# Padding the DRAM buffers between the two stages of an FFT convolution: 132 KB instead of 128 KB for each frequency pair

## The chip, the core and the metric

The kernel runs on one core of a Trainium2 chip. The metric is the device time of one execution in microseconds (us). Several runs are taken and the median is given. One further execution was recorded by the hardware profiler; the tables and lines of the profile come from that one.

## What is computed

```python
B, S, D = 8, 5696, 128                       # x: (B, S, D), h: (S, D), float32
Xf = np.fft.rfft(x, n=2 * S, axis=1)
Hf = np.fft.rfft(h, n=2 * S, axis=0)
y  = np.fft.irfft(Xf * Hf[None], n=2 * S, axis=1)[:, :S, :]
x  = y.reshape(B * S, D)                     # 45568 tokens
logits = x @ phi                             # phi: (128, 32), 8 experts with 4 slots
d = softmax of logits over the tokens; slot_input = d.T @ x
slot_out[e] = relu(slot_input[e] @ w1[e]) @ w2[e]
c = softmax of logits over the 32 slots;  out = c @ slot_out
```

It is a causal convolution along the sequence, done by a transform of twice the length, followed by a soft mixture of experts. All data are float32.

## The kernel before, in words

The sequence of 5696 tokens is seen as 89 rows of 64 columns. The transform has two factors, N1 = 90 and N2 = 64. It is applied to nine sequences in turn: first h (g = 0), then the eight batches of x (g = 1 to 8). Each sequence passes through three stages, and spectra travel between stages through DRAM.

**Stage A** (`load_x`, `fold`, `first_stage`) takes a chunk of 4 columns and their mirror image; NJ = 8 chunks make a sequence. `load_x` brings them in by two DMAs (80 rows and 9 rows). `fold` (line 206, GpSimd) forms sum and difference. `first_stage` multiplies by cosine and sine tables on TensorE (line 217), ScalarE copies the result from PSUM to the tile `fst` in SBUF (line 220, a ring of four), and SP stores it in DRAM (line 226). There are two shapes of stores. `first_low` holds two components of one chunk in partitions 0 to 63 and 64 to 127, of which 60 each are stored (two DMAs of 240 KB). `first_high`, in every odd step, holds two components of two chunks in four groups of 32 partitions, of which 30 each are stored (four DMAs of 120 KB). Each partition writes one run of 4 columns x 2 x 128 x 4 bytes = 4 KB.

**The DRAM buffer `fd[g]`** (line 131) holds the spectrum of one sequence after stage A: NP = 45 frequency pairs, in each pair 2 halves (`a`) of 64 columns (`r`), in each column 2 x 128 values. A column is 1 KB, a half 64 KB, a pair 128 KB. So the rows of one store, one for each half of each pair, are 64 KB apart. There are nine such buffers, one for each sequence, and none is used twice.

**Stage B** (`load_g`, `stage_b1`, `stage_b2`) transforms along the 64 columns. A unit is four pairs (NW = 12 units in a sequence, the last with one pair). `load_g` (line 253, SP) reads a unit into the tile `gt`, a ring of four: 128 partitions (half and column), 4 pairs, 1 KB each, 512 KB in all. TensorE multiplies (line 267), VectorE multiplies by the spectrum of h (lines 285 and 294), TensorE transforms back (line 309), ScalarE copies to `zst` (line 315), and SP stores it in `zd[b]` (line 318), which has the same pairs of 128 KB and is not changed.

**Stage C** (`load_pair`, `stage_c1` to `stage_c6`) reads 1 MB pieces of `zd` into `zc` (line 346), finishes the inverse transform (line 365), transposes (line 393), forms logits and keeps running sums of the softmax over tokens. After the last step the expert layers run and the output is written (lines 753 to 850).

**Order of the work.** It is written out by hand. One step of the main loop (line 583) handles one chunk of stage A, one or two units of stage B of the sequence before (LAG_B = 9 steps later) and, in every second step, one part of stage C (LAG_C = 27 steps later). Within a step two strings, `ORDER_E` and `ORDER_O` (line 581), give the order in which the pieces are issued: "x" loads x three steps ahead, "X" and "Y" are stage A with its stores, "p" and "P" prefetch units of stage B up to two steps ahead, "b" is a unit of stage B with its store, "z" loads for stage C. Nearly all DMAs are issued by SP, one after the other in this order; a DMA that has to wait holds up those behind it on SP. A load of a unit waits until all stores of the sequence that reach its pairs have landed.

Of the kernel before, what the change touches and what calls it, by code (L numbers as in the profile page):

```python
# [10 lines left out]
F32 = mybir.dt.float32  # L11
# [66 lines left out]
def kernel(  # L78
# [24 lines left out]
    nc = tc.nc  # L103
    P = 128
    B, S, D = x.shape
# [4 lines left out]
    N1, N2 = 90, 64  # L110
    R1, HALF, NP = S // N2, N2 // 2, N1 // 2
    CH = 4
# [15 lines left out]
    t_s1, t_i1, t_w, t_v, t_turn = [  # L128
        nc.inline_tensor(t, f"tab_{n}").ap()
        for n, t in zip(("s1", "i1", "w", "v", "turn"), transform_tables(S, N1, N2, CH, X0))]  # L130
    fd = [nc.dram_tensor(f"f_{g}", (NP, 2, N2, 2, D), F32, kind="Internal").ap() for g in range(B + 1)]
    zd = [nc.dram_tensor(f"z_{b}", (NP, 2 * N2, 2, D), F32, kind="Internal").ap() for b in range(B)]
    cd = nc.dram_tensor("c_t", (P, B * NQ, Q, 2, MH), F32, kind="Internal").ap()

# [38 lines left out]
    def bank():  # L173
        rings.append(rings.pop(0))
        return rings[-1].tile([P, 512], F32, name="bank", tag="bank")
# [34 lines left out]
    def first_stage(tiles, width):  # L210

        st = apool.tile([P, CH, 2, D], F32, name="fst", tag="fst", bufs=4)
        for G in range(2):
            p = bank()
            for o, (c, comp) in enumerate(tiles):
                k = slice(0, HP) if width == HP else slice(HP, HP + QP)
                nc.tensor.matmul(p[o * width:(o + 1) * width, :], s1[:, comp + G, k],  # L217
                                 folded[(c, comp)][:, :, :].rearrange("p n d -> p (n d)"),
                                 start=True, stop=True)
            nc.scalar.activation(st[:, :, G, :],  # L220
                                 p[:, :].rearrange("p (n d) -> p n d", d=D), AF.Copy)
        for o, (c, comp) in enumerate(tiles):
            g, j = divmod(c, NJ)
            n0 = comp * HALF + CH * j
            k0, n = (0, N1A) if width == HP else (N1A, N1 - N1A)
            nc.sync.dma_start(
                out=fd[g].rearrange("q a r c d -> (q a) (r c d)")[k0:k0 + n, n0 * 2 * D:(n0 + CH) * 2 * D],
                in_=st[o * width:o * width + n, :, :, :].rearrange("k n c d -> k (n c d)"))

    def first_low(c):  # L230
        first_stage([(c, comp) for comp in range(2)], HP)

    def first_high(c):

        both = [(c - 1 + i, comp) for i in range(2) for comp in range(2)]
        first_stage(both, QP)
        for b_ in both:
            del folded[b_]
# [3 lines left out]
    def parts(u):  # L242

        g, w = divmod(u, NW)
        return g, w, [(i, min(2, NP - 2 * i)) for i in range(2 * w, min(2 * w + 2, NU))]

    def load_g(u):
        if u >= (B + 1) * NW:
            return
        g, w, us = parts(u)  # L250
        n = sum(k for _, k in us)
        t_ = bpool.tile([P, 4, 2, D], F32, name="gt", tag="gt", bufs=4)
        nc.sync.dma_start(
            out=t_[:, 0:n, :, :].rearrange("p q c d -> p q (c d)"),
            in_=fd[g][4 * w:4 * w + n, :, :, :, :].rearrange("q a r c d -> (a r) q (c d)"))
        gs[u] = t_

    def stage_b1(u, share):
# [324 lines left out]
    for t in range(last_front + 1):  # L583
# [6 lines left out]
        def prefetch(last):  # L590
            nonlocal loaded
            while loaded < len(queue) and queue[loaded][1] <= last:
                load_g(queue[loaded][0])
                loaded += 1
# [58 lines left out]
        if NA < t <= NA + E:  # L653
# [13 lines left out]
                      in_=zring[0][held, :, :, :, :, :].rearrange("k h o n c d -> k (h o n c d)"))  # L667
# [16 lines left out]
    for q in range(Q):  # L684
        r = slice(q * NSL, (q + 1) * NSL)
        nc.gpsimd.tensor_copy(out=rep4[r, :, :],
                              in_=ident[r, r].unsqueeze(1).broadcast_to([NSL, Q, NSL]))
# [17 lines left out]
    for V in range(T, NT):  # L705
# [35 lines left out]
        else:  # L741
            for i in range(4 * (V - T - 1), min(4 * (V - T), E), 2):
                nc.sync.dma_start(
                    out=w2s[:, i:i + 2, :, :],
                    in_=moe_w2[i:i + 2].rearrange("e (p c) d -> p e c d", p=P))
# [39 lines left out]
    for g in range(EG):  # L785
        for k0 in range(0, NFC, 4):
            p = bank()
            for k in range(4):
# [3 lines left out]
                out=hidT[:, g, k0:k0 + 4, :], in_=p[:, :].rearrange("p (k c) -> p k c", k=4))  # L792
# [29 lines left out]
    for b in range(B):  # L822
        w1 = 0
        for n in (1, 2, 4, 4) if b == 0 else (4, 4, 3):
# [11 lines left out]
            for q in range(Q):  # L836
# [8 lines left out]
                out=ov[b, t0:t0 + n * RW * N2, :].rearrange("(w p n) d -> p w (n d)", p=P, n=CH),  # L845
                in_=o_[:, 0:n, :, :].rearrange("p w q d -> p w (q d)"))
            if lone:
                nc.sync.dma_start(
                    out=ov[:, NV * RW * N2:, :].rearrange("b (j n) d -> b j (n d)", n=CH),
                    in_=o_[:, n, :, :].rearrange("p q d -> p (q d)"))  # L850
# [29 lines left out]
```

## Time and profile before

| | |
|---|---|
| median of three runs | 871.69 us (867.33 to 872.01) |
| profiled execution, its own time | 869.39 us |
| its span, from first to last instruction | 867.6 us |
| mean granted TensorE clock | 0.947 of full speed |
| bytes moved by DMA | 272.46 MB, mean 314 GB/s |
| DMA pieces ("packets") | 156124, of which 113702 under 2 KB |
| HBM read, written | 142.81 MB, 128.21 MB |

How the profile is read: "busy" of an engine is the time in which it executed an instruction, and its share is of the span. A row of two dozen digits or more is the span in 40 equal slices, each digit the busy share in tenths, 9 for nine tenths or more. A group line gives the source line, the engine, the operation and the tiles as out<-in, then the number of instructions, then busy time and the mean of one. PEld is the loading of weights into TensorE, which overlaps with its matmuls (PE). The chain of work that ended last is followed back from the last instruction, at each step to what released it. "SPq" is SP's queue of instructions that issue DMAs; a DMA in the chain is the time from its issue to its landing.

The DMAs that touch the buffer, beside the largest others (KB each, number):

| DMA | number | KB each |
|---|---|---|
| f<-fst (line 226) | 144 and 144 | 240 and 120 |
| gt<-f (line 253) | 99 and 9 | 512 and 128 |
| z<-zst (line 318) | 88 and 8 | 512 and 128 |
| zc<-z (line 346) | 30, 90 and 30 | 1024, 128 and 32 |
| xc<-in_x_dram (line 195) | 64 and 64 | 320 and 36 |

### The profile page before, as it was taken

Reading aid. Unit: us, or ns where it says so; the run is one execution under the profiler, and the core shown is the slowest. Engines: PE = TensorE matmul, PEld = TensorE weight load, DVE = VectorE, ACT = ScalarE, POOL = GpSimd, SP = SyncE. Lnnn points to the kernel's source line nnn. Section 1 sums busy time; section 2 is a strip of 40 time slices with the busy share of each in tenths; the row PEclk is TensorE's granted clock in tenths of the full one; section 3 lists DMA queues with packets and bytes.
Section 4 is the critical chain, followed back from the end, with each engine's and each line's share of the span. In section 5 each row is a group of like instructions: output and inputs, shape, how many; then the busy total and the mean of one; then the engine's idle time right before and its main releaser. Section 6 shows DMA issues by size and latency. Waiting matters only on the chain.

```text
span 867.6 us, 20501 instructions
## 1 busy us (share of the span) xinstructions
PE 774.3 (89%) x7796; PEld 380.7 (44%) x7796; DVE 619.5 (71%) x929; ACT 442.6 (51%) x906; POOL 404.3 (47%) x386
## 2 busy tenths in 40 slices
PE   5889788889999999999999999999998888968993
PEld 1223333234444444444444444444454444444882
DVE  3049867667778778877888788777788895963642
ACT  2433244435555555655565565555544444773541
POOL 4453424245565566656566555555434332671000
PEclk9999999999999999999999999999999898988855
DMA  9899999999999999999999999999997886670898
GB/s 294 258 300 316 299 326 351 324 327 332 341 326 342 334 329 334 337 330 338 339 348 337 335 328 338 337 326 335 316 330 276 286 308 252 245 305 2 338 405 337
DMA packets 156124, 272.46 MB, mean 314 GB/s; under 512 B 12198, under 2 KB 113702, under 8 KB 152885
## 3 DMA queue, kind: packets, MB, share of 16 engines
q1 hardware_dynamic: 155451, 270.85, 90.2%
q8 instruction: 62, 1.02, 0.5%
q10 hardware_dynamic: 576, 0.31, 0.1%
q14 instruction: 35, 0.29, 0.1%
HBM read 142.81 MB, written 128.21 MB: 312 GB/s over the span
## 4 chain that ended last, share of the span: by engine, by line
PE 55%; DMA 20%; DVE 11%; SPq 2%; issue 2%; POOL 1%; ACT 1%; DVEq 0%; ACTq 0%
PE bank L365 13%; PE bank L217 11%; DMA zc<-z 8%; PE bank L309 7%; PE bt L267 7%; PE bank L393 6%; DMA out_dram<-o 4%; DMA xc<-in_x_dram 4%; DMA gt<-f 3%; DVE yf L294 3%; PE bank L480 3%; DVE p L285 2%; DVE bt L285 2%; SPq L346 2%; PE bank L431 2%
## 5 line engine op out<-in xcount | busy, mean ns | idle before, releaser
L206 POOL TENSOR_TENSOR x<-xc 128x512 f32<-128x512 f32 x144 | 180.1, 1275 | 228.5 <-PE bank L217 196.4
L217 PE MATMUL bank<-x,s 128*32 128x512 f32 (+1 forms) x1152 | 227.4, 613 | 16.3 <-POOL x L206 15.4
L315 ACT ACTIVATE zst<-bank 128x512 f32<-128x512 f32 (+1 forms) x184 | 98.7, 586 | 190.5 <-PE bank L309 168.8
L220 ACT ACTIVATE fst<-bank 128x512 f32<-128x512 f32 x216 | 127.5, 598 | 109.5 <-PE bank L217 85.0
L285 DVE TENSOR_TENSOR p<-bt,Hi 128x1024 f32<-128x1024 f32 x96 | 111.3, 1160 | 34.0 <-PE bt L267 33.1
L365 PE MATMUL bank<-zc,i 128*64 128x512 f32 x480 | 117.5, 611 | 10.8 <-DMA f<-fst 6.4
L309 PE MATMUL bank<-yf,vt 64*64 64x256 f32 x1440 | 102.4, 390 | 26.8 <-DVE yf L294 26.8
L217 PEld LDWEIGHTS bank<-x,s 128*32 128x32 f32 (+1 forms) x1152 | 57.0, 124 | 154.3 <-issue 76.1
L294 DVE TENSOR_TENSOR yf<-bt,p 128x512 f32<-128x512 f32 x192 | 119.3, 662 | 3.3
L267 PE MATMUL bt<-gt,wt 64*64 64x256 f32 x1620 | 113.7, 388 | 6.0 <-DMA gt<-f 3.9
L285 DVE TENSOR_TENSOR bt<-bt,Hr 128x1024 f32<-128x1024 f32 x96 | 112.9, 1177 | 0.0
L267 PEld LDWEIGHTS bt<-gt,wt 64*64 64x64 f32 x1620 | 54.0, 132 | 80.9 <-issue 38.0
L384 POOL TENSOR_TENSOR y<-y,op 128x512 f32<-128x512 f32 x64 | 77.5, 1211 | 11.4 <-DVE op L370 8.3
L309 PEld LDWEIGHTS bank<-yf,vt 64*64 64x64 f32 x1440 | 57.0, 135 | 58.0 <-issue 27.8
L370 DVE TENSOR_TENSOR y<-bank,y 128x512 f32<-128x512 f32 x32 | 22.1, 691 | 70.9 <-PE bank L365 70.6
L393 PE MATMUL bank<-ident,y 109*128 109x109 f32 x512 | 66.1, 283 | 0.7 <-DVE y L384 0.7
L384 POOL TENSOR_TENSOR y<-y,om 128x512 f32<-128x512 f32 x54 | 64.1, 1186 | 2.1
L365 PEld LDWEIGHTS bank<-zc,i 128*64 128x64 f32 x480 | 31.2, 137 | 74.6 <-issue 45.9
L393 PEld LDWEIGHTS bank<-ident,y 109*128 109x128 f32 x512 | 55.9, 154 | 16.5 <-issue 11.1
L395 ACT ACTIVATE yt<-bank 128x360 f32<-128x360 f32 x128 | 51.7, 489 | 4.2 <-PE bank L393 4.2
L833 PE MATMUL op<-so,cT 32*128 32x128 f32 x704 | 45.8, 378 | 3.6 <-ACT o L842 2.9
L285 DVE TENSOR_TENSOR p<-bt,turn 128x1024 f32<-128x1024 f32 (+1 forms) x12 | 14.2, 1179 | 46.6 <-PE bt L267 45.7
(97 smaller groups left out, 817.3 us busy)
## 6 DMA issues: line engine op xcount, KB each, us to landing
gt<-f SPq DMA_DIRECT2D x99, 512.0 KB
z<-zst SPq DMA_DIRECT2D x88, 512.0 KB
f<-fst SPq DMA_DIRECT2D x144, 240.0 KB
zc<-z SPq DMA_DIRECT2D x30, 1024.0 KB
xc<-in_x_dram SPq DMA_DIRECT2D x64, 320.0 KB
f<-fst SPq DMA_DIRECT2D x144, 120.0 KB
out_dram<-o SPq DMA_DIRECT2D x16, 1024.0 KB
zc<-z SPq DMA_DIRECT2D x90, 128.0 KB
```

Source lines behind the costliest of these rows:

```text
L206: nc.gpsimd.tensor_tensor(out=y_[:, :, :], in0=t_[:, 0, :, :], in1=t_[:, 1, ::-1, :], op=AL.subtract if comp else AL.add)
L217: nc.tensor.matmul(p[o * width:(o + 1) * width, :], s1[:, comp + G, k], folded[(c, comp)][:, :, :].rearrange("p n d -> p (n d)"), start=Tr ...
L220: nc.scalar.activation(st[:, :, G, :], p[:, :].rearrange("p (n d) -> p n d", d=D), AF.Copy)
L267: nc.tensor.matmul(bt[q * HP:(q + 1) * HP, a, o, :], wt[r, 2 * i + q, :], t_[r, 2 * o + q, :, :].rearrange("p c d -> p (c d)"), start=True ...
L285: nc.vector.tensor_tensor(out=p_, in0=pv, in1=h_, op=AL.mult)
L294: eng.tensor_tensor(out=y_[r, 0:k, c, :], in0=pv[:, :, c, :], in1=pi[r, 0:k, 1 - c, :], op=op_)
L309: nc.tensor.matmul(bz[q][a * HP:(a + 1) * HP, o * 2 * D:(o + 1) * 2 * D], vt[r, i, a, :], y_[r, a * m + o, :, :].rearrange("p c d -> p (c ...
L315: nc.scalar.activation(st[:, 0:m, q, :], bz[q][:, 0:m * 2 * D].rearrange("p (o x) -> p o x", o=m), AF.Copy)
L365: nc.tensor.matmul(p[h_ * HP:(h_ + 1) * HP, :], i1[0:kr, tab, :], t_[0:kr, h_, o, :, q, :], start=True, stop=True)
L384: eng.tensor_tensor(out=part_, in0=part(v, 0), in1=o_[:, :, :], op=sign)
L393: nc.tensor.transpose(p[:, i * TR:(i + 1) * TR], ys[T][0:TR, k * CH + i, 0:D], ident[0:TR, 0:TR])
L395: nc.scalar.activation(yt[:, k * CH:(k + 1) * CH, :, :], of_tokens(p), AF.Copy)
```

## The change

Each `fd[g]` is allocated with 4 more columns (4 KB) behind the 128 columns of each pair. The kernel works on the first 128 of each pair through a view; the 4 KB are never written or read. The distance from pair to pair becomes 132 KB. The distance between the halves of a pair stays 64 KB.

Because the two halves and the pairs no longer lie at one common distance, the destination of the stores in `first_stage` can't be written as one level of rows any more. It becomes two levels: pairs (30 for `first_low`, 15 for `first_high`) and halves (2), and then the run of 4 KB. The source in SBUF is written as before. The loads in `load_g` have halves and columns already joined in the view; their rows, pieces and sizes are the same. Nothing else is changed.

```diff
-    fd = [nc.dram_tensor(f"f_{g}", (NP, 2, N2, 2, D), F32, kind="Internal").ap() for g in range(B + 1)]
+    fd = [nc.dram_tensor(f"f_{g}", (NP, 2 * N2 + 4, 2, D), F32, kind="Internal").ap()[:, 0:2 * N2] for g in range(B + 1)]
...
             nc.sync.dma_start(
-                out=fd[g].rearrange("q a r c d -> (q a) (r c d)")[k0:k0 + n, n0 * 2 * D:(n0 + CH) * 2 * D],
+                out=fd[g].rearrange("q (a r) c d -> q a (r c d)", a=2)[
+                    k0 // 2:(k0 + n) // 2, :, n0 * 2 * D:(n0 + CH) * 2 * D],
                 in_=st[o * width:o * width + n, :, :, :].rearrange("k n c d -> k (n c d)"))
...
         nc.sync.dma_start(
             out=t_[:, 0:n, :, :].rearrange("p q c d -> p q (c d)"),
-            in_=fd[g][4 * w:4 * w + n, :, :, :, :].rearrange("q a r c d -> (a r) q (c d)"))
+            in_=fd[g][4 * w:4 * w + n, :, :, :].rearrange("q r c d -> r q (c d)"))
```

## Prediction

> **What bounds the kernel now.** I read the page first, then the stage table (busy time of each engine in chosen stretches), then the chain of work that ended last.
>
> ```profile
> span 867.6 us, 20501 instructions
> PE 774.3 (89%) x7796; PEld 380.7 (44%) x7796; DVE 619.5 (71%) x929; ACT 442.6 (51%) x906; POOL 404.3 (47%) x386
> DMA  9899999999999999999999999999997886670898
> ```
>
> Two resources look full: TensorE (89%) and the 16 DMA engines (nine tenths or more in most slices). The stage table shows which of them leads where. Its columns are the stretch and its length, busy us and instruction count of PE, PEld, DVE, ACT and POOL, then the granted clock, the DMA share and GB/s.
>
> ```profile
> 10.00:15.00 5.00, 5.00 (x15) 2.34 (x11) 0.00 (x0) 1.68 (x3) 2.00 (x2) 1.00 1.01 427
> 30.00:50.00 20.00, 16.38 (x73) 4.09 (x72) 0.00 (x0) 8.25 (x14) 11.00 (x9) 1.00 0.83 245
> 50.00:170.00 120.00, 101.61 (x906) 38.54 (x905) 93.17 (x106) 45.77 (x80) 45.01 (x36) 0.97 0.97 323
> 170.00:210.00 40.00, 34.54 (x298) 14.49 (x295) 25.91 (x36) 19.14 (x37) 18.94 (x17) 0.96 0.94 329
> 210.00:630.00 420.00, 412.86 (x4238) 191.74 (x4239) 332.78 (x514) 245.66 (x509) 240.35 (x223) 1.00 0.97 334
> 640.00:720.00 80.00, 67.08 (x741) 37.97 (x739) 69.40 (x108) 35.76 (x75) 27.41 (x28) 0.88 0.84 291
> ```
>
> From 210 to 630 us TensorE is busy 412.9 of 420 us: it sets the pace, and only 7.1 us are idle. The DMA share there is 0.97, so it just keeps up. From 50 to 210 us (the ramp, while the pipeline fills) TensorE is idle 160 - 101.6 - 34.5 = 23.9 us with the DMA share at 0.94 to 0.97. The last store to f is issued at 634 us, so nothing after about 700 us can be touched directly. The chain shows who leads in the ramp:
>
> ```profile
> 50.46 8.15 DMA xc<-in_x_dram
> 58.63 5.66 DMA gt<-f
> ...
> 74.41 7.89 DMA xc<-in_x_dram
> 82.37 5.42 DMA gt<-f
> ```
>
> Its share by line for 50 to 210 us is 19.9% loads of x, 16.9% loads gt<-f and 7.1% loads zc<-z: 44% of 160 us is 70 us of DMA in the chain. There the stores to f matter twice: they stand ahead of these loads on SP's one queue, and they share their DMA engines. Last, what issues cost (minimum, median, maximum in ns):
>
> ```profile
> L226 SPq DMA_DIRECT2D f<-fst x288: 314/362/1687, 13.9 to 634.3; - x144
> L253 SPq DMA_DIRECT2D gt<-f x108: 333/452/1426, 46.9 to 696.4; - x108
> ```
>
> **What the Trainium skill says.** (1) DMA: Bandwidth & Descriptors, Latency and other measured facts, row on HBM row pitch: copies of 16 KiB rows at a pitch of 512 KiB ran at 207 GB/s and at 4 MiB at 103; with 4 KiB added to the 4 MiB pitch 214. So the pad is of the size named there, but the pitch here is 64 KB in a pair and 128 KB between pairs, well under the one that lost only 3%. No view of this trace isolates such a loss. (2) The same page, Why a DMA increments its semaphore by 16 and not by 1: the number of engines is the largest number up to 16 that divides the slowest sizes of both sides. Before it is 60 and 60, and 30 and 30; after it 30 (pairs) and 60, and 15 and 30. All give 15, so the spread should not change. No view of the trace shows engines singly. (3) SBUF — State Buffer, Door 1: The DMA port swizzle: partitions 0 to 63 reach only 8 of 16 ports, and 1 MiB for 64 partitions was measured at 196 GB/s. This bears on a store whose 60 rows lie in one half of the partitions.
>
> Does the trace agree with (3)? In 30 to 50 us only x loads and f stores run. One round of two steps takes 8.89 us there (its first store is issued at 22.43, 31.32 and 40.21 us) and moves 0.73 MB of x and 1.47 MB of f. Busy time is 0.83 x 16 x 8.89 = 118 engine-us. At the 427 GB/s of the stretch that is full of table loads (26.7 GB/s for each engine) x would take 27. What is left, 91, over 360 pieces of 4 KB is about 252 ns a piece, where the table rate would give 153. Fifteen engines at 252 ns are 244 GB/s: stores to f are slow, and the 8 ports of (3), at 196 GB/s with the two halves partly overlapped, are enough to explain it. The pad does not touch ports.
>
> **The change part by part.** It removes nothing and adds no engine work, no bytes and no wait.
>
> (a) Stores (line 226, 288 of them). The pieces stay 60 or 30 of 4 KB. Their addresses go from multiples of 64 KB to pairs at 132 KB. Bounds of the unknown: if the pitch now costs as much as the page's 512 KiB (3% of 252 ns, 8 ns), the gain in the ramp is 87 stores (counted from their issues between 50 and 210 us) x 45 pieces on average x 8 ns / 16 = 2.0 us; if the new pitch is the worse one it is the same figure as a loss. With half of it on the path (44% of the ramp's chain is DMA) that is 0.9 us either way. I take -0.5 us, leaning to the page. From 210 to 630 us TensorE covers a gain, and a loss too as long as DMA slack lasts: 3% of a round of 20.3 us is 0.6 us, or 27 ns for each of the 22.5 pieces an engine has per round. Eight is below it.
>
> (b) Issue of the stores on SP. The destination gets a third level (pair, half, run) where it had two. No such row exists. The nearest is gt<-f with three levels: minimum 19 ns longer, median 90 ns longer, but it carries 512 pieces instead of 60. The lower end is nothing; a gain is excluded, since the pattern has no level fewer. I take 19 ns: 87 x 19 = 1.7 us in the ramp, half on the path 0.8 us; with 90 ns it is 3.9 us. In a round of the long stretch (456 to 476 us) SP's issues sum to about 16 us of 20.3, so eight stores at 19 or 90 ns more (0.2 or 0.7 us) lie in its 4 us of slack. Behind a store on SP stand the x load, z<-zst, and the zc and gt loads; a shift of 0.7 us meets loads that are issued one to two steps ahead.
>
> (c) Loads (line 253, 108 of them). The same 512 pieces of 1 KB, the same count on all levels; 128 rows on both sides before and after. Four pairs that were one run of 512 KB become four runs of 128 KB. Nothing in the page prices that; I take zero, with the same 3% as both ends. A piece may lengthen by 6.8 ns (0.6 us over 90 pieces an engine per round) before TensorE stops covering it.
>
> Sum: -0.5 + 0.8 = +0.3 us on the profiled execution, whose own time is 869.39 us (span 867.6 and 1.8 around it): 869.7. The median of the runs shown is 871.69, 2.3 above it, so +0.3 is 872.0 there; the part is smaller than the spread of the three runs (867.33 to 872.01). I put 871.5, between the two readings and near the median. The case's own range, with 90 ns and 3% against it or neither, is 867 to 877.
>
> **The rivals.**
>
> **Pitch relief is real.** The 252 ns come from addresses that all agree below 64 KB, not from ports. Then a piece could fall to the 153 ns of the table rate: 99 ns x 87 x 45 / 16 = 24 us of DMA time in the ramp, against 23.9 us of idle TensorE. Some of that idle is dependency (load, fold, matmul, store, load again), so I take half, 12 us, and 1 of the 7.1 us idle in the long stretch: 871.7 - 13 = 859. For it: 4 KB pieces are slower here than the 1 KB pieces that fill later stretches at 334 GB/s and 0.97. Against it: the ports explain it, and the page's loss at a larger pitch is 3%.
>
> **Issue on SP becomes the bound (slower).** The source names its 60 partitions in one level, the destination now in 30 x 2; if one issue has to do the work of two, a store costs 0.36 us more. In the ramp that is 87 x 0.36 = 31 us of SP time ahead of the x and gt loads that lead the chain; half of it on the path is 15.7 us. In the long stretch 8 x 0.36 = 2.9 us a round still fits in 4.3 us of slack, and it decides there from 0.54 us a store; below that I add nothing but 0.3 us at each of the seven batch boundaries, where a zc load leads the chain: 2 us. With 871.7 this gives about 889; with 0.2 us a store 881. From about 0.1 us a store it leaves the band of no change. For it: DMA in the ramp is already late, and the order on SP is fixed. Against it: gt<-f issues three levels at 333 ns at best.
>
> **The change does less than it says**: a base address elsewhere spreads the same pieces the same way, which ends in the first case.
>
> **How the numbers follow.** Chances: no change 0.53, pitch relief 0.17, SP issue 0.30. A measurement of this kernel can tell about 0.5% (4.4 us) from no change. The first case's upper end crosses +4.4 us with 0.04 of its chance and its lower end with 0.02: faster 0.19, same 0.47, slower 0.34. The range 860 to 885 leaves out the better half of the relief (0.08) and the dearer part of the SP case (0.12).
>
> **What would show it.** Right: issues of f<-fst within 20 ns of 362 and still 288 of them, the DMA share of 30 to 50 us at 0.83 with the same round of 8.89 us, the long stretch at 412 of 420 us, the x and gt loads of the ramp's chain at 5 to 8 us. Pitch relief would show as a lower DMA share at 30 to 50 us, and ramp loads in the chain of 4 to 6 us. The SP case would show as f<-fst issues of 0.5 us and more, or twice as many, and as x and gt loads issued later. I am wrong outright if store pieces slow by over 27 ns: then the DMA share goes to 1.0 and idle TensorE appears after 210 us.

## The result, and the profile after

The changed kernel takes 899.51 us (median of four runs, 899.14 to 901.91) against 871.85 us for the kernel before on the same chip: a ratio of 1.033, 95% interval 1.0285 to 1.0381, or some 28 us more. Medians here and below leave out the few runs in a slower state (of e10, for example, one run of 16, with 888.20 us and a clock of 0.936). The prediction was 871.5 us, within 860 to 885: wrong. The rival "issue on SP becomes the bound" had the right sign and, at 889 us, some 17 of the 28 us.

The page after, the lines that answer to those shown of before (the profiled execution took 901.91 us):

```profile
span 900.1 us, 20501 instructions
PE 777.7 (86%) x7796; PEld 380.0 (42%) x7796; DVE 619.9 (69%) x929; ACT 442.3 (49%) x906; POOL 403.7 (45%) x386
DMA  8789899999999999999999999999998977771798
```

The number of instructions is the same, TensorE's busy time is nearly the same (3.4 us more), and no engine works noticeably longer: nearly all of the added 32.5 us of span is idle time. The instructions that name f (minimum, median, maximum in ns, then first and last start) show what changed:

```profile
L226 SPq DMA_DIRECT2D f<-fst x288: 806/828/1437, 13.3 to 666.4; - x144
L254 SPq DMA_DIRECT2D gt<-f x108: 367/460/1722, 52.3 to 728.1; - x108
```

There are still 288 stores, but SP needs 828 ns to issue one where it needed 362, and never less than 806 where 314 was the least. The median issue of a gt load is much the same (460 ns against 452). The stage table of the changed kernel (columns as in the prediction):

```profile
30.00:50.00 20.00, 16.38 (x71) 3.96 (x70) 0.00 (x0) 7.87 (x14) 10.03 (x9) 1.00 0.78 225
50.00:170.00 120.00, 93.37 (x813) 34.56 (x816) 84.43 (x96) 42.51 (x74) 41.68 (x34) 0.94 0.93 299
170.00:210.00 40.00, 30.94 (x284) 12.65 (x278) 25.68 (x31) 15.83 (x30) 13.86 (x12) 0.91 0.96 323
210.00:630.00 420.00, 398.30 (x4072) 186.08 (x4076) 319.81 (x492) 235.17 (x486) 236.38 (x220) 1.00 0.96 319
```

TensorE is now idle for 21.7 of the 420 us from 210 to 630 us, where it was for 7.1, and for 35.7 of the ramp's 160, where it was for 23.9. Milestones place the loss: the first gt load is issued 5.4 us later (52.3 against 46.9), the first zc load 11.7 us later (181.0 against 169.3), the last store to f 32.1 us later (666.4 against 634.3), the end 32.5 us later. So about a third is lost before the long stretch and two thirds, 20 us, in it, some 0.9 us in each round.

In the first 50 us the cause can be seen directly. The issues of SP there, by start and duration (a row can join several issues and what lies between them), first before:

```profile
22.43 0.78 SPq L226 DMA_DIRECT2D f<-fst  x2
23.31 1.45 SPq L195 DMA_DIRECT2D xc<-in_h_dram  x2
24.89 3.89 SPq L226 DMA_DIRECT2D f<-fst  x6
28.88 0.71 SPq L195 DMA_DIRECT2D xc<-in_h_dram  x2
31.32 0.77 SPq L226 DMA_DIRECT2D f<-fst  x2
```

Then the changed kernel:

```profile
23.24 1.69 SPq L226 DMA_DIRECT2D f<-fst  x2
25.04 1.56 SPq L195 DMA_DIRECT2D xc<-in_h_dram  x2
26.70 5.24 SPq L226 DMA_DIRECT2D f<-fst  x6
32.05 0.87 SPq L195 DMA_DIRECT2D xc<-in_h_dram  x2
33.02 1.70 SPq L226 DMA_DIRECT2D f<-fst  x2
```

1.69 + 1.56 + 5.24 + 0.87 us and the small gaps between them fill the round of 9.8 us without a hole: SP is full. Before, the same rows took 0.78 + 1.45 + 3.89 + 0.71 = 6.8 us of a round of 8.89 us, and the 3.89 us hold a wait of 1.1 us for ScalarE's copies; the issues alone sum to some 5.5 us. In the long stretch SP is not full, but TensorE's waits show the loads coming late. Who waited for whom, over the whole span (total us, times, longest), first before and then in the changed kernel:

```profile
PE bank L365 <- DMA zc<-z: 3.9, 6, 1.3
PE bt L267 <- DMA gt<-f: 3.9, 4, 1.4
```

```profile
PE bank L366 <- DMA zc<-z: 26.0, 14, 5.1
...
PE bt L268 <- DMA gt<-f: 13.9, 7, 5.3
```

The two waits together grew by 32.1 us.

### The profile page after: what moved, and what is told of

Read it like the earlier page. It is cut to its first block, busy times and chain, and to the rows that moved or that the text cites. A ratio compares the mean times of both kernels' runs of the same rounds, so it can differ in the third digit from the quotient of the medians.

```text
span 900.1 us, 20501 instructions
## 1 busy us (share of the span) xinstructions
PE 777.7 (86%) x7796; PEld 380.0 (42%) x7796; DVE 619.9 (69%) x929; ACT 442.3 (49%) x906; POOL 403.7 (45%) x386
## 4 chain that ended last, share of the span: by engine, by line
PE 52%; DMA 21%; DVE 10%; SPq 8%; issue 2%; POOL 2%; ACT 2%; DVEq 0%; POOLq 0%; ACTq 0%
PE bank L366 13%; PE bank L217 11%; DMA zc<-z 10%; PE bank L310 7%; PE bt L268 6%; PE bank L394 6%; DMA out_dram<-o 4%; SPq L347 4%; SPq L226 3%; DMA xc<-in_x_dram 2%; DVE yf L295 2%; DMA gt<-f 2%; POOL x L206 2%; DVE p L286 2%; DVE bt L286 2%
## 5 line engine op out<-in xcount | busy, mean ns | idle before, releaser
L217 PE MATMUL bank<-x,s 128*32 128x512 f32 (+1 forms) x1152 | 224.9, 613 | 15.5 <-POOL x L206 14.5
L366 PE MATMUL bank<-zc,i 128*64 128x512 f32 x480 | 120.3, 623 | 29.7 <-DMA zc<-z 26.0
L394 PE MATMUL bank<-ident,y 109*128 109x109 f32 x512 | 64.6, 279 | 0.7 <-DVE y L385 0.7
L440 POOL MEMSET dt<- 64x8 f32 x32 | 3.4, 106 | 112.1 <-issue 54.6
```

Of the source, the lines that this page charges most:

```text
L366: nc.tensor.matmul(p[h_ * HP:(h_ + 1) * HP, :], i1[0:kr, tab, :], t_[0:kr, h_, o, :, q, :], start=True, stop=True)
L394: nc.tensor.transpose(p[:, i * TR:(i + 1) * TR], ys[T][0:TR, k * CH + i, 0:D], ident[0:TR, 0:TR])
```

## The experiments

**Theory S**: the padding itself does nothing; the two-level destination makes each issue dearer, and SP, which issues nearly all DMAs in one order, passes the delay on. **Theory A**: the new addresses make the pieces slower. Each kernel was timed beside the kernel before on the same chip (870.0 to 871.9 us, medians); ratios are to these.

The two compiled programs differ in one more thing, which gave the first experiment. The library marks a DMA as laid out beforehand when it can. The 288 stores carry the mark before the change (60 rows on both sides) and lose it by the change (60 rows against 30 x 2). A switch of the builder removes the mark without a change to the DMA.

**e1: the dear issue alone, no padding.**

```diff
+            nc.dge_precook = False
             nc.sync.dma_start(
                 out=fd[g].rearrange("q a r c d -> (q a) (r c d)")[k0:k0 + n, n0 * 2 * D:(n0 + CH) * 2 * D],
                 in_=st[o * width:o * width + n, :, :, :].rearrange("k n c d -> k (n c d)"))
+            nc.dge_precook = True
```

> The kernel before, unpadded, every address and every size as it was; only the 288 stores to f are issued the dearer way (the builder's switch for laying an issue out beforehand is off for them). Theory S (the stores' issue time on SP costs the time: 0.362 to 0.828 us a store gave +28 us, some 6 us for each 0.1 us): slower with no padding at all, by 6 us for each 0.1 us that the issue grows; with 0.55 us about 883 us, with 0.8 us about 898 us. Theory A (the new addresses make DMA pieces slower): 872 us, within 4 us.

Measured: 894.24 us, ratio 1.0295 (1.0237 to 1.0353), with these issues:

```profile
L227 SPq DMA_DIRECT2D f<-fst x288: 763/773/1585, 12.3 to 659.8; - x144
```

With every address as before, 0.41 us more for each store cost 23 us; the change had 0.47 us more and 28. Theory A gave 872 here: it can't account for more than the 5 us that are left.

**e2: the change with a pad of 64 KB** (`2 * N2 + 64` in place of `2 * N2 + 4`).

> The changed kernel with a pad of 64 KB behind each pair in place of 4 KB, so that the runs of one store agree in all address bits below 64 KB again, as before the change, while the stores are issued in the same two-level form. Theory S: 899 us within 4 us, issues of 0.83 us. Theory A: the 4 KB shift is gone, so back to 872 to 880 us.

Measured: 900.07 us (1.0335, 1.0298 to 1.0372), issues of 824 ns. The 4 KB shift is of no account, for worse or for better.

**e7 and e8: padding with cheap stores, and its control.** In e7 each half gets 2 KB behind it, so that rows lie 66 KB apart and a store keeps one level; the loads then need two DMAs. e8 has the two DMAs and no pad.

```diff
-    fd = [nc.dram_tensor(f"f_{g}", (NP, 2, N2, 2, D), F32, kind="Internal").ap() for g in range(B + 1)]
+    fd = [nc.dram_tensor(f"f_{g}", (NP, 2, N2 + 2, 2, D), F32, kind="Internal").ap()[:, :, 0:N2] for g in range(B + 1)]
...
-        nc.sync.dma_start(
-            out=t_[:, 0:n, :, :].rearrange("p q c d -> p q (c d)"),
-            in_=fd[g][4 * w:4 * w + n, :, :, :, :].rearrange("q a r c d -> (a r) q (c d)"))
+        for a in range(2):
+            nc.sync.dma_start(
+                out=t_[a * HP:(a + 1) * HP, 0:n, :, :].rearrange("p q c d -> p q (c d)"),
+                in_=fd[g][4 * w:4 * w + n, a, :, :, :].rearrange("q r c d -> r q (c d)"))
```

> The pad split between the halves: 2 KB behind each half of 64 KB, so that all rows of a store lie 66 KB apart and the store stays one level (cheap issue). The price is on the loads: each gt load is two DMAs of 64 partitions. To be read against the same loads without the pad (the next run). If the pad relieves the DMA: 5 us or more below that run, and a DMA share below 0.83 for the stretch in which only x loads and stores to f run. If addresses do not matter: equal within 5 us.

> The kernel before, unpadded, with each gt load as two DMAs of 64 partitions: the control of the run before. Theory S: 108 loads more to issue and 27 in place of 24 DMAs a round that wait for the one eight before; between 885 and 930 us. Without any role of SP: 872.

Measured: 982.07 us (1.1254, 1.1206 to 1.1303) and 982.50 us (1.1262, 1.1212 to 1.1311): equal within some 6 us, and both far slower than I expected. Before the first gt load only x loads and stores to f run; the stage table for 25 to 46 us, first of e7 (padded), then of e8:

```profile
25.00:46.00 21.00, 15.94 (x72) 3.87 (x70) 0.00 (x0) 7.79 (x14) 12.80 (x11) 1.00 0.84 263
```

```profile
25.00:46.00 21.00, 15.96 (x72) 3.88 (x70) 0.00 (x0) 7.90 (x14) 12.69 (x11) 1.00 0.84 262
```

The same DMA share and the same GB/s, with the stores cheap in both: at this pitch the padding does not change what a piece costs. Why 216 smaller loads in place of 108 cost some 112 us is taken up with e3.

**e9, e10, e17: half doses and another place.** The switch of e1 for the 144 stores of `first_high` only (e9), for the 144 of `first_low` only (e10), and for the 108 gt loads in place of the stores (e17).

> The kernel before, unpadded; only the 144 stores of first_high (four in a row in odd steps) are issued the dearer way, the 144 of first_low stay cheap. All 288 dear gave +23 us. Theory S (the sum of SP's issue time counts): half the dose, +12 us, about 883. Rival P (the place counts: in odd steps six stores stand in a row ahead of the zc and gt loads): nearly all of it, +18 to 23 us, about 892.

> The kernel before, unpadded; only the 144 stores of first_low (two in every step) are issued the dearer way. Theory S: +12 us, about 883. Rival P: little, 0 to 6 us, about 874.

> The kernel before, unpadded, cheap stores; the 108 gt loads are issued the dearer way in place of the stores. Theory S (any 0.1 us on SP for 288 issues is about 6 us, by the sum of SP time): 108 x 0.4 = 43 us of SP time against 118 for all stores (+23): +8 us, about 879. If dear issue hurts only where stores are concerned: 871 within 4 us.

Measured: 881.65 us (1.0108, 1.0072 to 1.0145), 877.84 us (1.0080, 1.0056 to 1.0105) and 874.95 us (1.0050, 1.0027 to 1.0073). The two halves, 11.7 and 7.9 us, add up to some 20 of the whole's 23. The dear loads cost less than I expected; their issues also grew less, by 0.24 us at the least value:

```profile
L254 SPq DMA_DIRECT2D gt<-f x108: 576/632/1649, 46.3 to 701.8; - x108
```

Taken by the least issue times and the medians of the runs, the added SP time and the loss are 142 us and 28 (the change), 129 and 23 (e1), 65 and 11.7 (e9), 65 and 7.9 (e10, both with e1's 0.45 us a store), 26 and 3.4 (e17): 0.12 to 0.2 us lost for each microsecond on SP. Rival P, that only the place of the stores counts, falls with e9 and e10; that stores of odd steps, ahead of the zc load, cost a little more is within the intervals. e17 does not decide: its 3.4 us fit this rate, but they also lie within the 4 us that I had allowed for dear loads that cost nothing, and the long stretch of its profiled execution shows no loss (TensorE busy 414.9 of 420 us, against 412.9 before):

```profile
210.00:630.00 420.00, 414.89 (x4280) 193.06 (x4276) 337.31 (x519) 247.63 (x512) 245.19 (x227) 1.00 0.97 334
```

**e15 and e16: room on SP.** All x and h loads are issued by GpSimd (`nc.gpsimd.dma_start` in `load_x`), without and with the change.

> The kernel before with all loads of x and h (144 DMAs) issued by GpSimd in place of SP. SP loses four issues of 0.36 us a round and GpSimd, busy 47%, gets them. 860 to 880; the control of the next run. Below 867 it would be a version better than both.

> The changed kernel (pad, dear stores) with the same loads issued by GpSimd. If SP's serial time in a round is what the dear stores overfill (theory S): with 20 in place of 24 DMAs on SP there is room again, and this run lies at most 10 us above the run before (the change against the kernel before is +28). If the dear form costs in another way, as by slower pieces on the DMA engines: still 22 to 30 above it.

Measured: 903.32 us (1.0392, 1.0314 to 1.0471) and 900.97 us (1.0354, 1.0281 to 1.0428). Loads by GpSimd are themselves a loss of 32 us (why was not examined), but on top of that the change costs nothing, within some 7 us, although its stores are as dear as ever. Its stores, first of e15 and then of e16:

```profile
L226 SPq DMA_DIRECT2D f<-fst x288: 314/405/2936, 20.6 to 665.4; - x144
```

```profile
L226 SPq DMA_DIRECT2D f<-fst x288: 798/823/3257, 19.9 to 666.2; - x144
```

And the stage table for the long stretch, in the same order:

```profile
210.00:630.00 420.00, 400.56 (x4019) 184.95 (x4020) 318.09 (x489) 234.18 (x484) 279.22 (x294) 0.98 0.99 318
```

```profile
210.00:630.00 420.00, 401.23 (x4021) 185.13 (x4019) 318.33 (x490) 234.57 (x485) 279.47 (x295) 0.98 0.99 318
```

With the DMA share at 0.99 in both, the DMA engines set the pace here, not SP, and the same 318 GB/s says that under this load neither the dear form nor the pad makes pieces slower to a degree that counts. The time of the dear issues is again taken from SP's waits: those that a DMA ended sum to 110.6 us in this stretch in e15 and to 64.6 us in e16.

Where SP issues the x loads, pieces did become slower, and not by the padding. The share and the rate say so for e1, whose addresses are those of before (0.97 and 334 GB/s before, 0.96 and 319 after):

```profile
210.00:630.00 420.00, 402.42 (x4100) 186.69 (x4096) 323.06 (x498) 236.94 (x490) 235.12 (x219) 0.99 0.96 321
```

The traces record every piece. From 210 to 630 us the pieces of 4 KB, nearly all of them of stores to f, took 174 ns on average before, 195 in the changed kernel and 194 in e1, with the same median of 159 ns in all three: it is a minority of pieces that became slower. 21 ns on 7645 pieces is 10 us on each of 16 engines. In e16 the pieces of SP's queue took 177 ns against 170 in e15, and nothing was lost, although the DMA engines were the bound. So under this load the form does not slow them by 21 ns. Whether the slower pieces carry a part of the 28 us, or only follow from stores that are issued at other times, was not separated.

**e3: two cheap issues for each store.** Unpadded, each store cut into two DMAs of half the rows.

> The kernel before, unpadded, with each store to f cut in two DMAs of half the rows (30 and 30, or 15 and 15): 576 cheap issues in place of 288, same addresses, same bytes. Theory S: two issues of about 0.36 us make 0.72 us a store, 0.36 us more, so about 893 us (885 to 900). Theory A: 872 us, within 4 us.

Measured: 965.37 us (1.1097, 1.1031 to 1.1162), more than four times the expected loss. SP's time is not what it cost: from 210 to 630 us its issues sum to 276 us here and to 313 us in e1, which lost 23 us. In the compiled program every DMA on SP waits until the one eight before it has landed. A round has 24 DMAs before, and 32 here for the same bytes, so eight in flight carry a quarter less. The long stretch agrees: the DMA share falls to 0.90, which e1, e2, e9 and e10 with their dear but undivided stores do not show (0.96 to 0.98).

```profile
210.00:630.00 420.00, 373.27 (x3669) 170.14 (x3665) 291.19 (x443) 212.33 (x437) 208.84 (x193) 0.95 0.90 290
```

That is an argument from the program and one number; the depth of eight was not varied. The same explanation would hold for e7 and e8 (27 in place of 24 DMAs a round, and each split load 0.6 us to issue, since a load of 64 partitions does not get the mark although its two sides have equal levels), but there the DMA share is 0.98 to 0.99 at 278 to 280 GB/s, so the pieces of these loads are slower on the DMA engines too. These parts were not separated.

**e5: the high stores of the changed kernel issued by ScalarE** (`nc.scalar.dma_start` when the width is that of `first_high`).

> The changed kernel with the 144 stores of first_high issued by ScalarE in place of SP; padding and addresses as in the change. Theory S: SP loses 144 x 0.83 = 119 us of issue work, back to about what it had before or less (4 x 0.83 = 3.3 us a round in place of 8 x 0.36 = 2.9), so 870 to 882 us, the upper part if ScalarE's own 3.3 us a round delays its copies out of PSUM. Theory A: 899 us, within 4 us.

Measured: 1024.52 us (1.1802, 1.1718 to 1.1885), a miss against both theories. ScalarE's program then holds four issues in a row, and SP's loads wait for them, because in the compiled program the DMAs of both engines take turns at the same eight semaphores. First a line of ScalarE's timeline, then what SP waited for; the x loads of line 195 read nothing that a store to f writes, and yet waited 90 us for these stores:

```profile
469.84 3.47 ACTq L226 DMA_DIRECT2D f<-fst  x4
```

```profile
SPq L254 <- DMA f<-fst: 94.5, 43, 8.0
SPq L195 <- DMA f<-fst: 90.0, 45, 7.0
```

It relieved SP of issue time and gave it waits of another kind, so it tells nothing about theory S. How much of the loss is ScalarE's own delay was not separated.

**e11 to e14: two more attempts to give SP room.** In e11 (changed kernel) and e12 (kernel before) the four stores of `first_high` are issued in the next step, behind its zc and gt loads. In e13 (before) and e14 (changed) a zc load is two DMAs in place of five.

```diff
-            "P": lambda: prefetch(t + 2),
+            "P": lambda: (prefetch(t + 2), [f() for f in held], held.clear()),
...
-    left = [(64 + 8 * j, min(8, n - 64 - 8 * j), j, 4) for j in range((n - 57) // 8)]
-    return [(0, 64, 32, 1)] + left
+    return [(0, 64, 32, 1), (64, n - 64, 0, 1)]
```

> The changed kernel (pad, dear stores), with the four stores of first_high issued one step later, behind the zc and gt loads of that step, in place of ahead of them. Same work, same issues. If the dear stores cost by standing ahead of the loads that TensorE waits for (zc <- z led nearly every round of the changed kernel's chain): 10 to 18 us of the 28 come back, 881 to 890. If only the sum of SP's issue time counts: 899 within 4 us.

> The kernel before with the same four stores one step later: the control of the run before. In the kernel before the loads were in time in the long stretch, so 871 within 5 us; below 867 would be a version better than both.

> The kernel before with each zc load in two DMAs in place of five (the last 26 rows lie in 26 neighbouring partitions): three issues of 0.6 us fewer on SP every second step. SP has slack in the long stretch there, so a gain only in the ramp: 864 to 871; slower, 875 or more, if 26 rows in neighbouring partitions move more slowly than three groups spread out.

> The changed kernel (pad, dear stores) with the same two zc DMAs in place of five. Theory S: SP gets back 3 x 0.6 = 1.8 us a round of the 8 x 0.47 = 3.7 us that the dear stores took, so about half of the loss, 28 us, returns: 880 to 890. If the loss had nothing to do with SP's issue time: 899 shifted only by what the run before shows.

Measured: 936.95 us (1.0742, 1.0680 to 1.0803), 890.03 us (1.0242, 1.0170 to 1.0313), 907.41 us (1.0434, 1.0386 to 1.0482) and 932.95 us (1.0726, 1.0667 to 1.0784). All four got slower, so neither arrangement helps, and the changed kernel lies 47 and 26 us above its control. In e13 the zc loads take the chain over; two of them there last longer than any of before (5.5 to 7.5 us in the long stretch):

```profile
449.09 8.36 DMA zc<-z
...
470.23 10.16 DMA zc<-z
```

Twenty-six rows in one DMA seem to move more slowly than the same rows in four DMAs that are spread over the partitions; it was not measured by itself. None of the fifteen kernels is faster than the kernel before.

## Why the prediction was wrong

**Where it held.** (a) The stores: the address change is worth nothing that can be seen either way. I gave it -0.5 us; e2 against the change and e7 against e8 put it at zero within some 6 us. What the Trainium skill has on the row pitch of DMA copies (page DMA: Bandwidth & Descriptors, Latency and other measured facts: half the rate lost at a pitch of 4 MiB, 3% at 512 KiB) agrees with no loss at 64 to 132 KB here. (c) The loads keep their price: their 1 KB pieces took 50 ns on average from 210 to 630 us, before and after. The rival "pitch relief" fell with e7 against e8. My 252 ns for a 4 KB piece was too high: in the records of the trace they took 210 ns on average from 25 to 46 us, before the first gt load. What is left of the excess over the table rate, which I had put down to the 8 ports of 60 partitions, is still unexplained by a run; only the pitch is excluded. The sign that I had named for being wrong outright, pieces slower by over 27 ns with the DMA share at 1.0, did not come: they slowed by 21 ns on average and the share stayed at 0.96, while TensorE did fall idle.

**The step that failed first: (b), the price of an issue.** "No such row exists. The nearest is gt<-f" was not true. The kernel before has one store whose two sides do not have the same levels, the very last (128 rows of the tile against 8 x 16 rows of the output, line 848), and its issue was in the trace:

```profile
L848 SPq DMA_DIRECT2D out_dram<-o x1: 1080/1080/1080, 855.9 to 855.9; - x1
```

I took 19 ns more, with 90 ns as the upper end, from a row that has three levels on both sides. What counts is not the number of levels but whether the DMA keeps the mark, and unequal levels lose it. With the mark an issue takes 292 to 367 ns at the least (loads of x, stores to f, gt loads); without it 527 (the zc loads, which lack it with equal levels), 576 (the gt loads of e17), 763 (e1) and 806 (the change). The term was 0.466 us in place of 0.019, 25 times what I took and five times my bound.

**The step that failed second: the cover in the long stretch.** I had 16 us of issues in a round of 20.3 and called the other 4 us slack, from which 8 x 0.36 = 2.9 us could be paid, with a threshold of 0.54 us a store. At 0.47 us, below the threshold, the long stretch lost 20 us. The 16 us were misread, for a row of the timeline also holds the waits between the issues that it joins. The issues alone sum to 256 us of the 420 from 210 to 630 us, or 12.4 us a round. So SP had some 8 us a round without an issue, twice what I took, and even these were not slack: most of them was SP waiting for DMAs to land. The waits of SP that a DMA ended summed to 130.2 us in that window before and to 66.1 us after, while its issues rose from 256 to 320 us. The added issue time came out of these waits nearly one for one, and time was lost all the same. The waits of SP for engines did not shrink (50 us before, 68 after), and TensorE waited longer for zc and gt loads. One of the waits, before and after:

```profile
SPq L318 <- DMA gt<-f: 23.8, 19, 2.2
```

```profile
SPq L319 <- DMA gt<-f: 10.9, 13, 1.6
```

A row of the before trace, over the whole span, that I could have read as a loan and not as slack:

```profile
SPq L195 <- DMA gt<-f: 38.9, 30, 2.0
```

TensorE was 98% busy there, the DMA engines 97%, and SP was nearly always issuing or waiting. My reading, which no run isolates, is that with three such queues in series a delay on one is not fully absorbed by the others; over the whole kernel 0.12 to 0.2 us came through for each microsecond.

**The ramp** was judged rightly in kind: 87 x 0.36 = 31 us of SP time, half on the path, was my rival's figure for a store 0.36 us dearer. With 0.49 us it would be 21 of 42 us. The first zc load came 11.7 us late, 5.4 of them from the first 50 us, so only some 6 of the 42 us came through. SP's waits for DMAs there went from 60.2 to 14.7 us, enough to take up the rest. In the first 50 us, where SP is full, about 1 us of the 3.7 us added to a round came through. So that this rival came near the measured total was in part luck: it had some 16 us in the ramp and 2 in the long stretch, where the traces show 12 and 20.

**What stays open.** The trace does not show what SP does in the added 0.47 us. That the stores' dear form costs the time, and not the padding, is shown (e1, e2, e7 with e8); that it costs through SP's serial time rests on e15 with e16 and on the doses, and the slower pieces are a rival for part of it. Nor was it shown which single wait carries the loss in the long stretch; among the 200 longest pieces of the chain 13 from 210 to 630 us are zc loads (78 us) where the kernel before has 8 (54 us), but the runs that meant to free this path changed other things as well.

## What to carry to other kernels

Before changing the layout of a DRAM buffer, write down the access pattern of both sides of each DMA and ask whether both still have the same levels (equal levels alone did not suffice for the zc loads and for the split loads of e8); look in the trace for any DMA that already has unequal ones and take its issue time. Free time on an issuing queue that consists of waits for landings is not slack to be spent one for one; if the engine that sets the pace is fed from that queue, price a delay there at some fraction and keep it in the range. And a padding that costs an issue form must first be shown to gain something: a pair of runs with and without the pad, at the same issue cost, answers that at once.

## What the runs showed of the hardware beyond expectation

- An issue of the same store from SP takes 0.36 us when it is laid out beforehand and 0.77 us when it is not (e1, medians); with a two-level destination against one level 0.83 us.
- Halving the size of the stores (e3) at 0.40 us an issue costs 94 us, far more than the issue time explains; the DMA engines' share falls to 0.90. Fewer bytes in eight DMAs in flight would explain it, which was not tested.
- Moving 144 issues of the changed kernel from SP to ScalarE (e5) cost a further 125 us; ScalarE was taken up by issues for 3.5 us at a time, and SP's loads waited 94.5 and 90.0 us for the stores.
- With dear stores the average 4 KB piece took 194 ns in place of 174, at the same addresses and the same median of 159 ns (e1).
